# Two heads' score products of the shared query tile on quarters of the TensorE array

## The chip, the core and the metric

One core of a Trainium2 chip runs the whole program. The metric is device time in microseconds (us), the median of several executions. The engines are TensorE (PE, with its weight loads shown apart as PEld), VectorE (DVE), ScalarE (ACT), GpSimd (POOL) and SyncE (SP), which issues the DMAs.

## The reference

Attention with pooled queries, then two feed-forward layers. Only the attention is touched by the change.

```python
B, H, S, D = q.shape                      # 2, 8, 1152, 64
q_pool = q.reshape(B, H, S // 2, 2, D).mean(axis=3)      # 576 queries a head
scores = q_pool @ k.transpose(0, 1, 3, 2) / sqrt(D)      # 576 x 1152 a head
attn = exp(scores - max); attn = attn / (sum + 1e-9)
x = attn @ v                              # tokens x 512 after the heads are joined
...
x = (P(h) / Q(h)) @ w_out,  h = x @ w_in                  # d_ff 2048
x = (silu(xn @ w_gate) * (xn @ w_val)) @ w_out2           # d_ff 1536, xn = rms norm of x
```

## The kernel before

**Pairs and tiles.** The 16 heads are worked in 8 pairs. A head has 576 queries, which are four full tiles of 128 and a rest of 64. The rests of both heads of a pair lie together in one *shared tile*, so a pair has 9 tiles: four of head 0, the shared one (t = 4), four of head 1. Over the kernel there are 72 tiles, numbered i = 9 pr + t; the shared ones are 4, 13, 22, 31, 40, 49, 58 and 67. `TILES` (lines 572 to 577) lists for each tile the heads whose queries it holds (`parts`, with the first column in `qT`) and where its columns go (`dests`).

**One tile.** Queries and keys stand transposed in `qT` and `kT`. A head has 64 dimensions, so `kT` has half of the key blocks on partitions 0 to 63 (row half 0) and the rest on 64 to 127 (row half 1), and `qT` has the queries on both. Step AB (`f_qk(0)`, line 748) makes four products of 64 rows by 128 columns, each with 256 moving columns: row half 1 into PSUM bank 1, row half 0 into bank 0, twice. Step C (`f_qk(1)`) makes one of 128 columns in row half 0 into bank 2. A float32 product is two matmul instructions, so a full tile is 8 and 2 matmuls on line 754, each with a weight load. Then DVE takes the row maximum over all three banks (line 783, "red" below; it depends on both AB and C), ACT the exponential (line 789, "exp"), PE transposes it in 64-row pieces back into the same PSUM tile (line 804: step T, and one piece, T2, which waits for the copy out of bank 0), and ACT or DVE copies it to `pt` (lines 836, 839). Once a head's tiles are done, nine accumulating steps "AV" (line 907) multiply by v, in two column halves of the array.

**The shared tile before.** Its weights are 128 columns for each head: head 0's 64 rest queries with 64 zero columns behind, head 1's with 64 zero columns ahead (`qn` was cleared there at line 559). Both heads' products accumulate into the same 128 PSUM partitions (`start` on the first, `stop` on the second), so the zeros keep the heads apart. That is 16 matmuls in AB and 4 in C.

**Order.** The order on PE in the attention is written out by hand (`seq`, lines 1001 to 1013). For two tiles a (even) and b (odd), a *slot* below, it is AB of a, T2 of the tile before, C of a, AB of b, C of b, up to five AV steps, T of a, T of b, T2 of a. Other PE work (transposes of k and q on line 702, of the reciprocals on 940 and 954) goes between by time. Even shared tiles (4, 22, 40, 58) fall in slots without AV, odd ones (13, 31, 49, 67) in slots with four AV steps. Everything else is ordered by a planner (`order`, line 329): each operation has an engine or a choice of engines, a price in ns, a key, and what it depends on; the planner plays the engines forward with these prices and for each engine issues the ready operation that can begin first, with the key deciding among those within 80 ns. Each engine then runs its queue in that order. The planner also fits in the conversion of the feed-forward weights (lines 171 to 232: on ACT, DVE and POOL) wherever an engine would be free. It prices AB at 870 and C at 220 for each head in the tile, so 1740 and 440 for a shared tile, and 100 for a change between the PE modes that it names `rows` and `columns`.

**After the attention**, the first feed-forward layer starts with projections of its first two units (line 498), planned together with the attention; the rest of both layers is planned by a second call of `order`.

Of the kernel before, what the change touches and what calls it, by code (L numbers as in the profile page):

```python
# [19 lines left out]
def attention_moe_moe2_kernel(  # L20
# [29 lines left out]
    HALF = SQ % 128  # L50
    NFULL = SQ // 128
# [14 lines left out]
    def T(tag, shape, dtype=F32, space=None):  # L66
        pool(tag, BUFS.get(tag, 1), space)
        return pools[tag].tile(shape, dtype, tag=tag, name=tag)
# [348 lines left out]
    PE, DVE, ACT, POOL = "PE", "DVE", "ACT", "POOL"  # L417
# [89 lines left out]
    def banked(accesses, g, ins, also=None):  # L507

        ins = ins.ins
        for o in range(3):  # L510
            for other in accesses[o]:
                if other.engine != ins.engine:
                    if o != g and other is not also:
                        tc.declare_no_dep(ins, other, reason="another bank")
                    else:
                        tc.add_manual_dep(ins, other.name, after, reason="the same bank")
        accesses[g].append(ins)
# [39 lines left out]
    tail = [slice(0, HALF), slice(HALF, 2 * HALF)]  # L557
# [12 lines left out]


    TILES = []
    for t in range(NFULL):
        TILES.append(([(0, t * 128)], [(0, t * 128, 0, 128)]))
    TILES.append(([(0, NFULL * 128), (1, 0)], [(0, NFULL * 128, 0, HALF), (1, NFULL * 128, HALF, HALF)]))
    for t in range(NFULL):
        TILES.append(([(1, (t + 1) * 128)], [(1, t * 128, 0, 128)]))
    NT = len(TILES)

    QW = SQ // 2  # L580
# [17 lines left out]
    def op_any(ways, key, deps=(), bufs=()):  # L598
        eng, c, fn = ways[0]
        return Op(eng, c, key, fn, deps, bufs, ways[1:])  # L600
# [9 lines left out]
    kT, qT, kT_op, qT_op, v_op, v_tile, kq_buf, v_buf = ({} for _ in range(8))  # L610
# [123 lines left out]
    def tile_ops(i):  # L734
        pr, t = divmod(i, NT)
        parts, dests = TILES[t]
        ps = s_ps[i % 2]
        key = i * TS
        e = {}
        nb, pb = Buf("nm"), Buf("p")  # L740
        if t == 0:
            sum_buf[pr] = Buf("sums")
        sb = sum_buf[pr]


        ORDER_QK = [[(1, 1, 0, 256), (0, 0, 0, 256), (1, 1, 256, 512), (0, 0, 256, 512)], [(0, 2, 512, 640)]]

        def f_qk(n_):
            fresh = {}
            for a, j, x0, x1 in ORDER_QK[n_]:  # L750
                rows = slice(64 * a, 64 * a + 64)
                c = x0 % 512
                for n, (h, c0) in enumerate(parts):
                    ins = nc.tensor.matmul(  # L754
                        ps[:, j, c:c + x1 - x0],
                        lhsT=qT[2 * pr + h][rows, c0:c0 + 128],
                        rhs=kT[2 * pr + h][rows, x0:x1],
                        start=(n == 0),
                        stop=(n == len(parts) - 1),
                    )  # L760
                    banked(bank[i % 2], j, ins)
                    fresh.setdefault(j, []).append(ins.ins)
            for j in fresh:
                bank[i % 2][j][:] = fresh[j]

        deps, bufs = [], []
        for h, c0 in parts:
            deps += kT_op[2 * pr + h]
            deps += [o for (x0, x1), o in qT_op[2 * pr + h] if x0 < c0 + 128 and x1 > c0]
            bufs += kq_buf[2 * pr + h]  # L770
        o_qk = []
        for n_, (js, c) in enumerate((((0, 1), 870), ((2,), 220))):
            free = [o for j in js for o in lo_op.get((i - 2, j), ())]
            o_qk.append(Op(PE, c * len(parts), key + n_, lambda n_=n_: f_qk(n_), [*deps, *free], bufs))
            o_qk[-1].mode = "rows"
        tile_pe[i] = {"AB": o_qk[0], "C": o_qk[1]}

        def scores():
            return ps.rearrange("p g n -> p (g n)")[:, 0:S]

        def f_red():
            e["nm"] = T("nm", [128, 1])
            nc.vector.tensor_reduce(out=e["nm"], in_=scores(), op=ALU.max, axis=AX.X, negate=True)  # L783

        def f_exp():
            if pr not in sums:
                sums[pr] = T("sums", [128, NT])
            e["p"] = T("p", [128, S])
            nc.scalar.activation(  # L789
                e["p"], scores(), AF.Exp, bias=e["nm"], scale=1.0, accum_out=sums[pr][:, t:t + 1]  # L790
            )

        o_red = Op(DVE, 1350, key + -2500, f_red, o_qk, [nb])
        o_exp = Op(ACT, 1430, key + 2400, f_exp, [o_red], [nb, pb, sb])
        sum_op.setdefault(pr, []).append(o_exp)

        NB = NKT - 1

        def one_T(r, j, also=None):
            g, c = (2, 64 * r) if j == NB else (r, 64 * j)
            rows = slice(64 * r, 64 * r + 64)
            ins = nc.tensor.transpose(ps[:, g, c:c + 64], e["p"][rows, 128 * j:128 * j + 128], ident[rows, rows])  # L804
            banked(bank[i % 2], g, ins, also)

        def f_T():
            one_T(1, NB)
            for j in range(NB):
                one_T(0, j)  # L810
                one_T(1, j)

        def f_T2():
            one_T(0, NB, e["copied"].ins)


        OUTS = [(0, slice(0, NB), 0), (1, slice(0, NB), 1), (2, slice(NB, NKT), None)]

        def f_out(n_, copy):
            g, js, half = OUTS[n_]  # L820
            src = ps[:, g, 0:64 * NB if half is not None else 128]
            for h, o, s0, n in dests:
                if (pr, h) not in pt:
                    pt[pr, h] = T("pt", [128, NKT, SQ])
                to = pt[pr, h][:, js]
                if half is None:
                    banked(bank[i % 2], g, copy(to[:, 0, o:o + n], src[:, s0:s0 + n]))
                elif s0 <= 64 * half < s0 + n:
                    o_ = o + 64 * half - s0
                    ins = copy(to[:, :, o_:o_ + 64], src.rearrange("p (j n) -> p j n", n=64))  # L830
                    banked(bank[i % 2], g, ins)
                    if g == 0:
                        e["copied"] = ins

        def by_act(to, src):
            return nc.scalar.activation(to, src, AF.Copy)  # L836

        def by_dve(to, src):
            return nc.vector.tensor_copy(to, src)  # L839

        o_T = Op(PE, 560, key, f_T, [o_exp], [pb])
        o_T.mode = "rows"
        for h, *_ in dests:
            if (pr, h) not in pt_buf:
                pt_buf[pr, h] = Buf("pt")
        for n_ in range(3):
            half = OUTS[n_][2]
            hs = [h for h, o, s0, n in dests if half is None or s0 <= 64 * half < s0 + n]
            w = 64 * NB if half is not None else 128
            n2 = 150 * (len(hs) - 1)  # L850
            done = op_any(
                [(ACT, 70 + 1.09 * w + n2, lambda n_=n_: f_out(n_, by_act)), (DVE, 80 + 1.16 * w + n2, lambda n_=n_: f_out(n_, by_dve))],
                key + 3300 + 300 * n_, [o_T if half is not None else o_T2], [pt_buf[pr, h] for h in hs],
            )
            if n_ == 0:
                o_T2 = Op(PE, 60, key + 300, f_T2, [done], [pb])
                o_T2.mode = "rows"
                tile_pe[i].update(T=o_T, T2=o_T2)
            lo_op[i, OUTS[n_][0]] = [done]
            for h in hs:  # L860
                pt_op.setdefault((pr, h), []).append(done)
# [168 lines left out]
    for u in FINE:  # L1030
        free = [o for g in range(3) for o in lo_op[NP * NT - 2 + u, g]]
# [463 lines left out]
```

## Time and profile before

| | |
|---|---|
| median of 3 executions | 757.92 us (756.67 to 759.8) |
| the profiled execution's own time | 756.91 us |
| its span from first to last instruction | 755.1 us |
| mean granted TensorE clock | 0.988 |
| attention stage, to where line 498 begins on PE | about 291 us |
| matmul instructions on line 754 | 800, 160 of them in the 8 shared tiles |

The profile is of one execution, and durations are read from it; 1.8 us of its time lie outside the span. A matmul's end is modelled, so starts are more exact than ends. A timeline row merges neighbouring instructions of one kind and gives their start, how long they took together and their count (x16). "[1.80 <-PE hid L754]" says that the engine sat idle 1.80 us before that row, and what ended the wait.

### The profile page before, as it was taken

Reading aid. Unit: us, or ns where it says so; the run is one execution under the profiler, and the core shown is the slowest. Engines: PE = TensorE matmul, PEld = TensorE weight load, DVE = VectorE, ACT = ScalarE, POOL = GpSimd, SP = SyncE. Lnnn points to the kernel's source line nnn. Section 1 sums busy time; section 2 is a strip of 40 time slices with the busy share of each in tenths; the row PEclk is TensorE's granted clock in tenths of the full one; section 3 lists DMA queues with packets and bytes.
Section 4 is the critical chain, followed back from the end, with each engine's and each line's share of the span. In section 5 each row is a group of like instructions: output and inputs, shape, how many; then the busy total and the mean of one; then the engine's idle time right before and its main releaser. Section 6 shows DMA issues by size and latency. Waiting matters only on the chain.

```text
span 755.1 us, 13099 instructions
## 1 busy us (share of the span) xinstructions
PE 704.8 (93%) x5257; PEld 613.3 (81%) x5257; DVE 561.4 (74%) x713; ACT 402.9 (53%) x641; POOL 279.5 (37%) x247
## 2 busy tenths in 40 slices
PE   7998889898989999889999989889999999999997
PEld 6766666666666767889989989888999899989996
DVE  5799998888898763887896777967758435864844
ACT  4666767776776663998764835605523322312210
POOL 3033645655674000434432352316435223512500
PEclk9999999999999999999999999999999999999999
DMA  6443656566562110222203204000123302330103
GB/s 204 142 134 120 184 174 219 192 222 191 192 223 86 50 52 2 72 96 94 74 29 125 94 6 140 29 28 1 43 98 112 111 29 85 113 111 29 56 1 125
DMA packets 51596, 77.13 MB, mean 102 GB/s; under 512 B 4176, under 2 KB 33872, under 8 KB 51536
## 3 DMA queue, kind: packets, MB, share of 16 engines
q1 hardware_dynamic: 51536, 76.30, 31.2%
q8 instruction: 41, 0.67, 0.4%
q14 instruction: 19, 0.16, 0.1%
HBM read 61.87 MB, written 14.42 MB: 101 GB/s over the span
## 4 chain that ended last, share of the span: by engine, by line
PE 60%; DVE 20%; ACT 9%; issue 7%; POOL 2%; DMA 1%; SPq 0%; DVEq 0%; POOLq 0%; ACTq 0%
PE hid L498 24%; PE accp L498 16%; PE hid L754 7%; PE av L907 6%; PE hid L804 4%; ACT p L789 3%; DVE nm L783 3%; DVE pt L839 2%; DVE m_p L1131 1%; DVE m_q L1110 1%; DVE wc L176 1%; PE prep L702 1%; DVE wc L186 1%; DVE wc L180 1%; ACT m_p L1097 1%
## 5 line engine op out<-in xcount | busy, mean ns | idle before, releaser
L498 PE MATMUL hid<-x_hi,win_hi 128*128 128x384 f32 x480 | 162.3, 338 | 5.8 <-issue 2.7
L498 PE MATMUL hid<-x_lo,win_hi 128*128 128x384 f32 x480 | 161.5, 336 | 0.0
L498 PE MATMUL hid<-x_hi,win_lo 128*128 128x384 f32 x480 | 161.2, 336 | 0.0
L754 PE MATMUL hid<-kT,qT 64*128 64x256 f32 (+1 forms) x800 | 107.4, 377 | 2.8 <-DVE pt L839 2.3
L789 ACT ACTIVATE p<-hid,nm 128x1152 f32<-128x1152 f32 x72 | 87.8, 1221 | 37.4 <-DVE nm L783 37.3
L783 DVE TENSOR_REDUCE nm<-hid 128x1 f32<-128x1152 f32 x72 | 94.6, 1349 | 13.5 <-PE hid L754 12.6
L498 PEld LDWEIGHTS hid<-x_hi,win_hi 128*128 128x128 f32 x480 | 90.6, 189 | 8.7 <-issue 5.6
L754 PEld LDWEIGHTS hid<-kT,qT 64*128 64x128 f32 x800 | 86.0, 194 | 10.2 <-DVE pt L839 4.2
L498 PEld LDWEIGHTS hid<-x_lo,win_hi 128*128 128x128 f32 x480 | 90.7, 189 | 1.2 <-DVE x_lo L1303 0.3
L498 PEld LDWEIGHTS hid<-x_hi,win_lo 128*128 128x128 f32 x480 | 90.7, 189 | 0.0
L804 PEld LDWEIGHTS hid<-ident,p 64*128 64x128 f32 x1296 | 53.1, 141 | 40.4 <-ACT p L789 23.5
L804 PE MATMUL hid<-ident,p 64*128 64x64 f32 x1296 | 67.7, 232 | 16.4 <-ACT p L789 14.5
L1145 POOL TENSOR_TENSOR g_lo<-m_p,g_hi 128x1152 fp32r<-128x1152 f32 (+1 forms) x20 | 47.0, 2358 | 88.0 <-ACT g_hi L1142 88.0
L498 PE MATMUL accp<-g_hi,wout_hi 128*128 128x384 f32 x192 | 66.1, 344 | 11.5 <-DVE acc L1200 10.0
L907 PE MATMUL av<-pt,vn 128*64 128x288 f32 x576 | 76.7, 411 | 0.0
L836 ACT ACTIVATE pt<-hid 128x512 f32<-128x512 f32 (+2 forms) x132 | 54.5, 438 | 33.3 <-PE hid L804 32.2
L839 DVE COPY pt<-hid 128x512 f32<-128x512 f32 (+1 forms) x92 | 54.4, 607 | 20.4 <-PE hid L804 20.1
L171 ACT ACTIVATE wc<-wraw 128x512 f32<-128x512 f32 x68 | 45.9, 675 | 38.9 <-POOL wout_lo L204 17.2
L199 POOL TENSOR_SCALAR win_hi<-wc 128x512 fp32r<-128x512 f32 x25 | 16.1, 645 | 134.4 <-PE hid L498 105.7
L498 PE MATMUL accp<-g_lo,wout_hi 128*128 128x384 f32 x192 | 64.9, 338 | 0.2 <-POOL g_lo L1145 0.2
L498 PE MATMUL accp<-g_hi,wout_lo 128*128 128x384 f32 x192 | 64.7, 337 | 0.0
L907 PEld LDWEIGHTS av<-pt,vn 128*64 128x64 f32 x576 | 38.6, 136 | 26.3 <-issue 1.0
(121 smaller groups left out, 1277.7 us busy)
## 6 DMA issues: line engine op xcount, KB each, us to landing
wraw<-in_moe_w_out_dram SPq DMA_DIRECT2D x28, 512.0 KB, 3.5
far<-spill SPq DMA_DIRECT2D x23, 512.0 KB, 3.7
wraw<-in_moe_w_in_dram SPq DMA_DIRECT2D x16, 512.0 KB, 4.2
wraw<-in_moe_w_gate_dram SPq DMA_DIRECT2D x12, 512.0 KB, 3.6
wraw<-in_moe_w_val_dram SPq DMA_DIRECT2D x12, 512.0 KB, 3.9
kn<-in_k_dram SPq DMA_DIRECT2D x16, 288.0 KB, 3.8
vn<-in_v_dram SPq DMA_DIRECT2D x16, 288.0 KB, 3.0
qn<-in_q_dram SPq DMA_DIRECT2D x16, 256.0 KB, 3.3
```

The costliest lines, as they stand in the source:

```text
L171: nc.scalar.activation(c.bitcast(F32), wt["raw", n][:, :, 1].bitcast(F32), AF.Abs, scale=2.0**-112)
L176: nc.vector.tensor_scalar(c, c, 3, None, op0=ALU.logical_shift_left)
L199: eng.tensor_scalar(hi, w_float(n), 1.0, 1.0, op0=ALU.mult, op1=ALU.mult)
L498: ins = nc.tensor.matmul(dst, lhsT=a[x], rhs=b[y], start=first and i == 0 and p == 0, stop=last and i == n - 1 and p == 2,)
L754: ins = nc.tensor.matmul(ps[:, j, c:c + x1 - x0], lhsT=qT[2 * pr + h][rows, c0:c0 + 128], rhs=kT[2 * pr + h][rows, x0:x1], start=(n == 0), ...
L783: nc.vector.tensor_reduce(out=e["nm"], in_=scores(), op=ALU.max, axis=AX.X, negate=True)
L789: nc.scalar.activation(e["p"], scores(), AF.Exp, bias=e["nm"], scale=1.0, accum_out=sums[pr][:, t:t + 1])
L804: ins = nc.tensor.transpose(ps[:, g, c:c + 64], e["p"][rows, 128 * j:128 * j + 128], ident[rows, rows])
L836: return nc.scalar.activation(to, src, AF.Copy)
L839: return nc.vector.tensor_copy(to, src)
L907: nc.tensor.matmul(e["av", h][64 * c:64 * c + 64, 0:QW], lhsT=v_tile[2 * pr + h][:, KEYS[kt], :], rhs=pt[pr, h][:, kt, c * QW:(c + 1) * QW ...
L1145: eng.tensor_sub(g_(1), p_(), g_(0).bitcast(F32))
```

## The change

In the shared tile each head's weights are cut to its own 64 columns, and each head's product goes to its own 64 PSUM partitions: head 0 to partitions 0 to 63, head 1 to 64 to 127. With the two row halves that addresses four quarters of the array (64 rows by 64 columns each). There is no accumulation over the heads any more; every product starts and stops by itself. Full tiles keep 128 columns (`whole`). The number of instructions stays the same: 16 matmuls in AB and 4 in C. The planner's price of AB and C no longer grows with the number of heads. The hand-written order `seq` is not touched, and the mode name stays `rows`.

```diff
     TILES = []
+    whole = slice(0, 128)
     for t in range(NFULL):
-        TILES.append(([(0, t * 128)], [(0, t * 128, 0, 128)]))
-    TILES.append(([(0, NFULL * 128), (1, 0)], [(0, NFULL * 128, 0, HALF), (1, NFULL * 128, HALF, HALF)]))
+        TILES.append(([(0, t * 128, whole)], [(0, t * 128, 0, 128)]))
+    TILES.append(([(0, NFULL * 128, tail[0]), (1, HALF, tail[1])], [(0, NFULL * 128, 0, HALF), (1, NFULL * 128, HALF, HALF)]))
     for t in range(NFULL):
-        TILES.append(([(1, (t + 1) * 128)], [(1, t * 128, 0, 128)]))
+        TILES.append(([(1, (t + 1) * 128, whole)], [(1, t * 128, 0, 128)]))
...
-                for n, (h, c0) in enumerate(parts):
+                for h, c0, to in parts:
                     ins = nc.tensor.matmul(
-                        ps[:, j, c:c + x1 - x0],
-                        lhsT=qT[2 * pr + h][rows, c0:c0 + 128],
+                        ps[to, j, c:c + x1 - x0],
+                        lhsT=qT[2 * pr + h][rows, c0:c0 + to.stop - to.start],
                         rhs=kT[2 * pr + h][rows, x0:x1],
-                        start=(n == 0),
-                        stop=(n == len(parts) - 1),
+                        start=True,
+                        stop=True,
                     )
...
-            o_qk.append(Op(PE, c * len(parts), key + n_, lambda n_=n_: f_qk(n_), [*deps, *free], bufs))
+            o_qk.append(Op(PE, c, key + n_, lambda n_=n_: f_qk(n_), [*deps, *free], bufs))
```

## Rows read from the trace of the kernel before

**Rows 1.** The page: span, and the chain that ended last, by engine.
```profile
span 755.1 us, 13099 instructions
...
PE 60%; DVE 20%; ACT 9%; issue 7%; POOL 2%; DMA 1%; SPq 0%; DVEq 0%; POOLq 0%; ACTq 0%
```

**Rows 2.** Busy time by stretch: attention, and all that follows.
```profile
0.00:291.00 291.00, 263.78 (x2849) 194.98 (x2850) 241.60 (x340) 196.76 (x387) 122.40 (x136) 0.98 0.48 155
291.00:755.10 464.10, 441.07 (x2409) 418.33 (x2408) 319.79 (x373) 206.19 (x255) 157.10 (x112) 0.99 0.21 69
```

**Rows 3.** Groups by line: score products and AV, with their weight loads.
```profile
L754 PE MATMUL hid<-kT,qT 64*128 64x256 f32 (+1 forms) x800 | 107.4, 377 | 2.8 <-DVE pt L839 2.3
...
L907 PE MATMUL av<-pt,vn 128*64 128x288 f32 x576 | 76.7, 411 | 0.0
...
L907 PEld LDWEIGHTS av<-pt,vn 128*64 128x64 f32 x576 | 38.6, 136 | 26.3 <-issue 1.0
```

**Rows 4.** PE's timeline in three slots: shared tile 4, full tiles, shared tile 67.
```profile
20.11 2.05 PE L754 MATMUL hid<-kT,qT 64*128 64x256 f32 x16
22.01 0.22 PE L804 MATMUL hid<-ident,p 64*128 64x64 f32 x1
22.06 1.75 PE L754 MATMUL hid<-kT,qT 64*128 64x128 f32 x14
23.74 0.66 PE L702 MATMUL prep<-ident,kn 128*128 128x128 f32 x4
25.57 0.77 PE L804 MATMUL hid<-ident,p 64*128 64x64 f32 x17 [1.17 <-ACT p L789]
...
30.39 2.65 PE L907 MATMUL av<-pt,vn 128*64 128x288 f32 x20
...
35.75 1.63 PE L754 MATMUL hid<-kT,qT 64*128 64x256 f32 x12
37.31 2.16 PE L907 MATMUL av<-pt,vn 128*64 128x288 f32 x16
...
269.25 1.08 PE L754 MATMUL hid<-kT,qT 64*128 64x256 f32 x8
270.21 0.27 PE L804 MATMUL hid<-ident,p 64*128 64x64 f32 x1
270.30 2.63 PE L754 MATMUL hid<-kT,qT 64*128 64x256 f32 x22
272.86 2.16 PE L907 MATMUL av<-pt,vn 128*64 128x288 f32 x16
```

**Rows 5.** DVE's timeline at shared tiles 4, 22, 31, 40, 58, 67.
```profile
22.82 2.62 DVE L783 TENSOR_REDUCE nm<-hid 128x1 f32<-128x1152 f32 x2 [1.80 <-PE hid L754]
...
97.42 2.62 DVE L783 TENSOR_REDUCE nm<-hid 128x1 f32<-128x1152 f32 x2 [0.33 <-PE hid L754]
...
130.49 1.36 DVE L783 TENSOR_REDUCE nm<-hid 128x1 f32<-128x1152 f32 x1 [0.89 <-PE hid L754]
...
169.63 1.52 DVE L219 SCALAR_TENSOR_TENSOR wc<-wraw,wc 128x512 uint32<-128x512 uint32 x1
171.06 2.61 DVE L783 TENSOR_REDUCE nm<-hid 128x1 f32<-128x1152 f32 x2
...
242.74 2.62 DVE L783 TENSOR_REDUCE nm<-hid 128x1 f32<-128x1152 f32 x2 [0.24 <-PE hid L754]
...
270.79 1.36 DVE L783 TENSOR_REDUCE nm<-hid 128x1 f32<-128x1152 f32 x1 [0.64 <-PE hid L754]
273.02 1.36 DVE L783 TENSOR_REDUCE nm<-hid 128x1 f32<-128x1152 f32 x1 [0.87 <-PE hid L754]
```

**Rows 6.** ACT's timeline at shared tile 31.
```profile
132.52 0.82 ACT L588 ACTIVATE xt<-av 64x288 f32<-64x288 f32 x2 [0.99 <-PE av L907]
...
134.02 1.23 ACT L789 ACTIVATE p<-hid,nm 128x1152 f32<-128x1152 f32 x1
```

**Rows 7.** Busy time and granted clock (third from the end) around tile 22; PE's timeline there.
```profile
93.00:96.00 3.00, 3.00 (x27) 2.81 (x25) 2.47 (x4) 1.32 (x3) 2.01 (x3) 0.50 0.88 306
...
93.61 3.22 PE L754 MATMUL hid<-kT,qT 64*128 64x256 f32 x16
```

More of the change, by code (lines that the diff above doesn't have):

```diff
@@ L766, in tile_ops @@
         deps, bufs = [], []
-        for h, c0 in parts:
+        for h, c0, to in parts:
             deps += kT_op[2 * pr + h]
-            deps += [o for (x0, x1), o in qT_op[2 * pr + h] if x0 < c0 + 128 and x1 > c0]
+            deps += [o for (x0, x1), o in qT_op[2 * pr + h] if x0 < c0 + to.stop - to.start and x1 > c0]
             bufs += kq_buf[2 * pr + h]
```

## The prediction

> **What bounds the kernel now.** I read the page first. The chain that ended last is 60% PE, 20% DVE and 9% ACT [rows 1], so no one engine sets the time alone. The busy times by stretch split it: up to 291 us, where the attention ends, PE is busy 263.8 us and DVE 241.6; in the 464 us behind, PE is busy 441 [rows 2]. The change touches only the attention, and whatever it saves there moves the start of a stage that it does not touch. In the attention the work passes from engine to engine: scores on PE, maximum on DVE, exponential on ACT, transposes on PE, copies on DVE and ACT. PE waits for the exponential (1.17 us ahead of T of tile 4 [rows 4]) and DVE waits for the scores (1.80 us in the same slot [rows 5]). So I do not price the change by PE's busy time but slot by slot, by what the maximum and the transposes wait for there.
>
> The groups by line show what a product costs [rows 3]: 800 matmuls of the scores with 107.4 us between them, the 8 shared tiles holding 160 of them. PE's timeline shows one shared tile beside full ones [rows 4]. In the slot of tile 4, AB of the shared tile starts at 20.11 and T2 behind it at 22.01: 1.90 us. In the slot of tile 66, a full one, it is 270.21 - 269.25 = 0.96. The shared tile pays for two heads one after the other in each half of the array's rows.
>
> **The change part by part.**
>
> *AB and C in quarters.* Removed: no instruction; 16 and 4 matmuls stay. What can change is how many run side by side. Today 8 further matmuls cost 1.90 - 0.96 = 0.94 us, 0.12 us each, with two row halves running together. Whether column halves run together too is seen in AV, which uses two of them: 20 matmuls take 2.65 us, 16 take 2.16 [rows 4], so one costs (2.65 - 2.16)/4 = 0.12 us, while its mean duration is 411 ns [rows 3]. It streams 288 columns where the score product streams 256, at the same price per instruction, so two column halves run together as two row halves do. The trace has no product on a quarter. The bounds: four quarters together make AB of the shared tile as long as that of a full tile, 0.96; if the column halves take turns, it stays at 1.90. The nearest row is AV's, so I take the first, about 1.0.
>
> *Even shared tiles (4, 22, 40, 58).* DVE's maximum for tile 4 starts 22.82 - 20.11 = 2.71 us after its AB [rows 4, 5]; for full tile 66, where DVE also waited for PE, 270.79 - 269.25 = 1.54. The difference, 1.17 us, is what the second head costs on this path (0.94 in AB, the rest in C). On PE alone less is gained, since C of an even tile shares the array with AB of the odd one behind it: the 14 matmuls from 22.06 take 23.74 - 22.06 = 1.68 until the next work, the 12 of a full slot 37.31 - 35.75 = 1.56.
>
> *Odd shared tiles (13, 31, 49, 67).* From C of the even tile to the first AV there are 22 matmuls and 272.86 - 270.30 = 2.56 us; a full slot has 12 and 1.56 [rows 4]. The second head costs 1.00 us on the path through AV to T.
>
> *Added: changes of the array's shape.* T2 and full tiles run on 64*128, the quarters on 64*64. Where the shape changes today, the next block starts 0.07 us ahead of the modelled end of the block before (22.06 + 1.75 = 23.81 against 23.74); where it stays, 0.15 us ahead (20.11 + 2.05 = 22.16 against 22.01) [rows 4]. That is 0.08 us. On top the new block has to fill: AV's 20 matmuls take 2.65 where 20 x 0.1225 is 2.45, so 0.2 us for start and end together. A change costs between 0.08 and 0.28; I take 0.15. An even shared tile has four changes, three of them ahead of its maximum (before AB, between AB and T2, between T2 and C); an odd one has one more than today, since AV follows it with a change anyway.
>
> *The sum.* Even: 1.17 - 3 x 0.15 = 0.72. Odd: 1.00 - 0.15 = 0.85. Four of each make 6.3 us; without the price of the changes it would be 8.7.
>
> *Whether the slots give it back.* This depends on DVE's queue. If each queue kept its order, a tile would gain no more than the wait in front of its maximum [rows 5]: tile 4 its 0.72 (of 1.80), tile 22 0.33, tile 31 0.85 (of 0.89), tile 58 0.24, tile 67 0.85 (of 0.87), and tiles 13, 40, 49 nothing, because DVE ran a weight conversion up to the maximum (tile 40: line 219 for 1.52 us until the maximum at 171.06; the other two look like it). That makes 3.0 us. But these conversions stand there because the planner saw a hole: it prices the shared scores at 1740 + 440. With 870 + 220 the maximum is ready when it looks, and the conversion goes to another hole; DVE has 291 - 242 = 49 us of them [rows 2]. The same holds for ACT at tile 31: the maximum was done at 131.85, yet the exponential begins at 134.02, behind two copies that waited for AV until 132.52 [rows 6]. With the lower price it can be issued ahead of them, worth up to 134.02 - 131.85 = 2.17 us by itself in such a slot. So 3.0 is the floor while the quarters work, and 8.7 about the ceiling. I take 6 us, close to the sum. What is late next: in even slots the copy out of bank 0 that T2 waits for, in odd ones the maximum of the even tile ahead of that of the shared one on DVE (1.36 us each).
>
> *The new prices elsewhere.* All orders of DVE, ACT and POOL in the attention are planned anew, and the second layerwise plan starts from the engines' new end times. No row prices that; I put it into the range. One event can be priced: a stretch at half clock. Around tile 22 the granted clock is 0.50, the lower of the two levels, 1.2 GHz, and the same 16 matmuls take 3.22 us in place of 2.05 [rows 7], 1.17 more. One such stretch more or less moves the time by about that.
>
> *The sum against its own time.* The profiled execution took 756.91, so 750.9; the median shown is 757.92, 1.0 above it, so 751.9 for the measured median. I predict 752.
>
> *A rule of the skill that speaks against it.* AV's weight loads take 136 ns and its matmuls follow each other at 0.1225 us with two running at once [rows 3, 4]; ten pairs with the load waited for would take 10 x (0.245 + 0.136) = 3.8 us, and the row has 2.65. The Trainium skill, "TensorE: Matmul & The Clock Gate", Part 3 (The mechanism), says that a weight load overlaps running matmuls only when its row group differs from theirs, and the two heads of one row half share it. The trace disagrees for column halves over all rows; no row shows it for quarters. What it would do here is the second rival.
>
> **The rivals.**
>
> *1. The quarters do not run together.* The row halves do, the column halves take turns, and AB stays at 1.90. Then only the changes of shape are new: four in an even tile and one in an odd one, 5 x 0.15 x 4 = 3.0 us, so 761. For it: the trace has no 64*64 product. Against it: AV.
>
> *2. Quarters run together, but each load waits for the running matmuls of its row half.* Each quarter has four passes of 0.94/4 = 0.235 us; each would pay 136 ns more, 0.54 us a tile. Even tiles keep 0.72 - 0.54 = 0.18, odd ones 0.85 - 0.54 = 0.31: 2.0 us, 756.
>
> *3. Slower: all four quarters in turn.* If products on quarters lose the overlap of the row halves as well, 16 passes of 0.235 take 3.8 us in place of 1.90, in C nothing changes, and with the changes of shape it is 8 x 1.9 + 3 = 18 us: 776. Its place is AB of the shared tile, and it decides by 0.5% once AB takes more than 1.90 + (3.8 - 3.0)/8 = 2.0 us. Against it: rows and columns overlap separately today.
>
> *4. The gain is made and given back by the new order.* Conversions that leave the holes of tiles 13, 40 and 49 land in front of another maximum or delay the copies. For it: DVE is busy 83% of the attention. Worth up to the 6 us: 756 to 759. Against it: the weights' keys rank them behind the tiles' own work when both are ready.
>
> **How the numbers follow.** A measurement of this kernel tells about 0.5%, 3.8 us, from no change. My case has a chance of 0.64: a gain of 3.0 to 8.7, 749 to 755. A larger gain through the reordered exponentials, 743 to 749, has 0.08. Rival 1 has 0.05, rival 2 0.08, rival 3 0.04, rival 4 0.11. Faster by over 0.5% (below 754.1) takes 0.59 of the first and the 0.08, 0.67. Slower (above 761.7) takes rival 3, half of rival 1 and 0.02 of rival 4, 0.09. The rest, 0.24, is the same. The range of 746 to 759 leaves out about 0.07 below and 0.12 above.
>
> **What would show it.** In the trace after, the shared tile's matmuls carry 64*64, AB with 16 of them lasts near 1.1 us, and T2 behind tile 4 starts about 1.2 us after AB in place of 1.90. The waits of DVE for line 754 shrink (1.80 in the slot of tile 4 to about 1.1), line 219 no longer stands in front of the maximum of tile 40, and line 498 begins on PE near 285 us. AB still near 1.9 means rival 1; 64*64 matmuls a load apart, rival 2; AB near 3.8, rival 3; AB short but line 498 still near 290, rival 4. The prediction is also wrong if the feed-forward stage does not simply start earlier but changes its own 464 us.

## The result

The changed kernel takes 746.95 us (median of 5 executions, 745.29 to 748.49) against 759.26 for the kernel before beside it (median of 5); the ratio is 0.9841, 95% interval 0.9817 to 0.9866. It is faster by about 12 us, twice the 6 forecast, and at the lower end of the range of 746 to 759. The profiled execution took 745.6 us with a span of 743.8, 11.3 less than before. Below, medians and ratios are of the fast executions alone: two of the twelve of the quarters in the old order (761.38 and 762.03 us), one of the quarters at the price halfway (1122.02) and one of the kernel before (865.72) are slow ones and stand in neither.

The page of the kernel after gives its span and the chain that ended last by engine, as [rows 1] did:

```profile
span 743.8 us, 13108 instructions
...
PE 62%; DVE 20%; ACT 9%; issue 6%; POOL 2%; DMA 1%; SPq 0%; DVEq 0%; POOLq 0%; ACTq 0%
```

Busy time by stretch, cut again where line 498 begins on PE (columns as in [rows 2]):

```profile
0.00:279.50 279.50, 257.62 (x2849) 185.42 (x2849) 236.20 (x350) 196.95 (x379) 123.09 (x133) 0.98 0.50 161
279.50:743.80 464.30, 441.35 (x2409) 418.62 (x2409) 320.06 (x374) 206.48 (x255) 157.51 (x113) 0.99 0.21 69
```

All of it comes from the attention, 11.5 us by these cuts; the 464 us behind it only start earlier. PE is busy 6.2 us less in the attention than in [rows 2], and DVE 5.4 less. The quarters cannot explain DVE: it has no less to do with them. This is the first sign that something else came along.

PE's timeline after, in the slots of shared tiles 13 and 58 (lines behind the edit stand one lower, 755 for 754). The 22 matmuls are two of tile 12 and all twenty of tile 13:

```profile
52.40 0.27 PE L805 MATMUL hid<-ident,p 64*128 64x64 f32 x1
52.51 1.68 PE L755 MATMUL hid<-kT,qT 64*128 64x128 f32 x22
54.12 2.16 PE L908 MATMUL av<-pt,vn 128*64 128x288 f32 x16
...
228.88 1.09 PE L755 MATMUL hid<-kT,qT 64*64 64x256 f32 x16
230.03 0.27 PE L805 MATMUL hid<-ident,p 64*128 64x64 f32 x1
230.23 1.72 PE L755 MATMUL hid<-kT,qT 64*64 64x128 f32 x14
231.88 0.66 PE L703 MATMUL prep<-ident,kn 128*128 128x128 f32 x4
```

AB of tile 58 is 16 matmuls on 64*64 in 1.09 us, where 16 on 64*128 took 2.05 and the 8 of a full tile 1.08 [rows 4]: four products run side by side. In the odd slot it is 54.12 - 52.51 = 1.61 us from C of the even tile to AV, against 2.56 before and 1.56 in a full slot [rows 4].

DVE's timeline at shared tiles 4, 13, 40 and 58, for [rows 5]:

```profile
24.37 2.62 DVE L784 TENSOR_REDUCE nm<-hid 128x1 f32<-128x1152 f32 x2 [1.70 <-PE hid L755]
...
53.55 2.61 DVE L784 TENSOR_REDUCE nm<-hid 128x1 f32<-128x1152 f32 x2
...
160.88 0.88 DVE L840 COPY pt<-hid 128x512 f32<-128x512 f32 x2
161.68 2.76 DVE L784 TENSOR_REDUCE nm<-hid 128x1 f32<-128x1152 f32 x2
...
230.14 0.76 DVE L605 TENSOR_TENSOR x_lo<-xt,x_hi 128x576 fp32r<-128x576 f32 x1 [0.16 <-POOL x_hi L592]
230.81 2.62 DVE L784 TENSOR_REDUCE nm<-hid 128x1 f32<-128x1152 f32 x2
```

The conversion on line 219 no longer stands in front of the maximum of tile 40, and the two maxima of slot 12 (a slot is named by its first tile) follow each other (x2 in one row). Tile 4 still waits 1.70 us. A part of that is the clock: it is 0.50, the lower level of 1.2 GHz, from 20.0 to 23.3 us, and the 16 matmuls take 1.78 us there in place of 1.09. Without these 0.69 us the wait would be about 1.0, by this estimate, where 1.1 was forecast. Busy time with the granted clock, and PE's row:

```profile
20.00:23.30 3.30, 2.96 (x43) 2.04 (x39) 1.38 (x2) 1.95 (x5) 0.00 (x0) 0.50 0.92 274
...
21.91 1.78 PE L755 MATMUL hid<-kT,qT 64*64 64x256 f32 x16
```

ACT's timeline at shared tile 31, for [rows 6]: the exponential of tile 31 comes right behind that of tile 30, ahead of the copies that wait for AV.

```profile
124.74 1.22 ACT L790 ACTIVATE p<-hid,nm 128x1152 f32<-128x1152 f32 x1
125.85 0.20 ACT L790 ACTIVATION_READ_ACCUMULATOR p<-hid,nm 128x1 f32 x1
125.94 1.23 ACT L790 ACTIVATE p<-hid,nm 128x1152 f32<-128x1152 f32 x1
```

### The profile page after: what moved, and what is told of

Its sections match the earlier page's. It is cut to its first block, busy times and chain, and to the rows that moved or that the text cites. A ratio compares the mean times of both kernels' runs of the same rounds, so it can differ in the third digit from the quotient of the medians.

```text
span 743.8 us, 13108 instructions
## 1 busy us (share of the span) xinstructions
PE 699.0 (94%) x5257; PEld 604.0 (81%) x5257; DVE 556.3 (75%) x723; ACT 403.4 (54%) x633; POOL 280.6 (38%) x245
## 4 chain that ended last, share of the span: by engine, by line
PE 62%; DVE 20%; ACT 9%; issue 6%; POOL 2%; DMA 1%; SPq 0%; DVEq 0%; POOLq 0%; ACTq 0%
PE hid L498 22%; PE accp L498 16%; PE hid L755 9%; PE av L908 8%; PE hid L805 4%; DVE nm L784 2%; DVE pt L840 2%; ACT p L790 2%; DVE m_p L1132 2%; DVE m_q L1111 1%; DVE wc L186 1%; PE prep L703 1%; DVE m_q L1126 1%; ACT m_p L1098 1%; DVE wc L180 1%
## 5 line engine op out<-in xcount | busy, mean ns | idle before, releaser
L790 ACT ACTIVATE p<-hid,nm 128x1152 f32<-128x1152 f32 x72 | 87.7, 1220 | 31.0 <-DVE nm L784 30.5
L755 PE MATMUL hid<-kT,qT 64*128 64x256 f32 (+3 forms) x800 | 99.9, 383 | 3.8 <-DVE pt L840 3.3
L755 PEld LDWEIGHTS hid<-kT,qT 64*128 64x128 f32 (+1 forms) x800 | 75.4, 185 | 14.1 <-DVE pt L840 4.7
L805 PE MATMUL hid<-ident,p 64*128 64x64 f32 x1296 | 69.2, 234 | 12.5 <-ACT p L790 10.1
L498 PE MATMUL accp<-g_hi,wout_hi 128*128 128x384 f32 x192 | 66.1, 344 | 11.3 <-DVE acc L1201 9.9
L840 DVE COPY pt<-hid 128x512 f32<-128x512 f32 (+2 forms) x94 | 51.7, 567 | 18.4 <-PE hid L805 18.1
```

The lines of the kernel that those rows point to most:

```text
L498: ins = nc.tensor.matmul(dst, lhsT=a[x], rhs=b[y], start=first and i == 0 and p == 0, stop=last and i == n - 1 and p == 2,)
L755: ins = nc.tensor.matmul(ps[to, j, c:c + x1 - x0], lhsT=qT[2 * pr + h][rows, c0:c0 + to.stop - to.start], rhs=kT[2 * pr + h][rows, x0:x1], ...
L790: nc.scalar.activation(e["p"], scores(), AF.Exp, bias=e["nm"], scale=1.0, accum_out=sums[pr][:, t:t + 1])
```

## The experiments

The diff does two things: it moves the products to quarters, and it lowers two prices of the planner, by which the other queues are ordered. The first question was which of the two brings the 12 us.

**Quarters alone, in the old order.** The changed kernel with the old price. The queues of DVE, ACT and POOL are then operation for operation those of the kernel before.

```diff
-            o_qk.append(Op(PE, c, key + n_, lambda n_=n_: f_qk(n_), [*deps, *free], bufs))
+            o_qk.append(Op(PE, c * len(parts), key + n_, lambda n_=n_: f_qk(n_), [*deps, *free], bufs))
```

> The quarters with the planner's old price (1740 and 440 for the shared tile), so that DVE, ACT and POOL have the order of the kernel before, operation for operation. Theory A (the quarters and the lower price each bring a part): only the waits in front of the maximum shrink, the forecast's floor of 3.0 us, so 3 to 5 us faster than before, the attention ending near 287 us. Rival B (the quarters bring it all, whatever the order): 11 to 12 us faster, the attention ending near 279. Rival C (the gain comes from another order of the queues and the quarters are worth nothing by themselves): within 1 us of before, near 291.

Measured: 754.45 us, ratio 0.9969 (0.9946 to 0.9991), 2.3 us faster. In its profile the attention ends at 286.3 (290.8 in the kernel before). Rival B falls. The 2.3 is just under theory A's 3 to 5 and the forecast's floor of 3.0, but it was measured at a lower clock than the kernel before had, which the next run takes up. DVE's timeline in the slots of tiles 13 and 40 shows what the old order leaves in the way:

```profile
53.34 1.34 DVE L784 TENSOR_REDUCE nm<-hid 128x1 f32<-128x1152 f32 x1
54.61 0.96 DVE L176 TENSOR_SCALAR wc<-wc 128x512 uint32<-128x512 uint32 x1
55.60 0.69 DVE L180 SCALAR_TENSOR_TENSOR wc<-wraw,wc 128x512 uint32<-128x512 uint32 x1
56.21 1.35 DVE L784 TENSOR_REDUCE nm<-hid 128x1 f32<-128x1152 f32 x1
...
167.89 1.52 DVE L219 SCALAR_TENSOR_TENSOR wc<-wraw,wc 128x512 uint32<-128x512 uint32 x1
169.33 2.61 DVE L784 TENSOR_REDUCE nm<-hid 128x1 f32<-128x1152 f32 x2
```

The conversions stand where the planner saw a hole, and the maximum waits behind them although its scores are ready.

**The new order alone.** The kernel before with the new price: serial products, queues as in the kernel after.

```diff
-            o_qk.append(Op(PE, c * len(parts), key + n_, lambda n_=n_: f_qk(n_), [*deps, *free], bufs))
+            o_qk.append(Op(PE, c, key + n_, lambda n_=n_: f_qk(n_), [*deps, *free], bufs))
```

> The products of before (128 columns, the two heads one after the other) with the planner's new price (870 and 220), so that DVE, ACT and POOL have the order of the kernel after. Theory A: the order is made for scores that now come about 1 us later in each of 8 tiles, and the maximum stands in the queue with nothing in front of it; the order still moves weight conversions out of the way, so the attention ends 3 to 5 us before 291, 286 to 288. Rival B (only the quarters count): no gain, 290 to 292, or a loss of some us. Rival C (only the order counts): near 280, 10 us or more faster.

Measured: 753.66 us, ratio 0.9949 (0.9932 to 0.9966), 3.9 us faster with not one product changed, as theory A had it. 2.3 and 3.9 make 6.2; together they bring 12.1.

Most of that gap goes with the clock. The executions of the quarters in the old order had a mean granted clock of 0.980, the kernel before beside them 0.987, the new price alone and both together 0.986. Where it was alike, the quarters in the old order took 749.92 us against 755.24 to 755.58 (at 0.991) and 754.14 against 760.84 (at 0.982), 5.5 and 6.7 us less. At 0.986 the new price alone took 753.25 against 757.81 (means of 5 and 8 executions), 4.6 less, and both together, in another session, 746.82 (mean of 4), 11.0 less. By these few executions the two parts about add up.

What DVE has to do goes with the order. Busy time of the attention, the quarters in the old order first, then the new order alone:

```profile
0.00:286.30 286.30, 258.21 (x2848) 183.61 (x2848) 241.56 (x340) 196.39 (x387) 122.48 (x135) 0.98 0.49 157
```

```profile
0.00:287.50 287.50, 265.36 (x2849) 196.69 (x2849) 236.77 (x350) 196.92 (x379) 122.71 (x133) 0.98 0.48 157
```

The third busy time is DVE's: 241.6 with 340 instructions in the old order, as in [rows 2], and 236.8 with 350 in the new. The planner chose other engines for some operations, and some take less time each where they now run: DVE has line 605 (604 in the second kernel) 6 times at a mean of 1116 ns in the old order, 5 times at 833 in the new.

**One column half.** As the changed kernel, with both heads' 64 columns in the same half of the array's columns.

```diff
-    TILES.append(([(0, NFULL * 128, tail[0]), (1, HALF, tail[1])], ...
+    TILES.append(([(0, NFULL * 128, tail[0]), (1, HALF, tail[0])], ...
```

> As the changed kernel, but head 1's 64 columns go to the same column half as head 0's, so that two quarters run at a time and not four; what lands on PSUM partitions 64 to 127 of the shared tile is then old data, so a part of the output is not the reference's. Same orders as the changed kernel. Theory A (the four quarters side by side are what shortens the scores): AB of the shared tile takes 1.8 to 1.9 us again, and the time is that of the new price alone within 1 us. Rival D (narrower weights or the lack of accumulation over the heads do it): AB stays near 0.95 us, and the time is that of the changed kernel.

Measured: 755.02 us, ratio 0.9972 (0.9952 to 0.9992), 1.4 above the new order alone (753.66), where 1 was expected. PE's timeline at tile 58:

```profile
231.16 2.00 PE L755 MATMUL hid<-kT,qT 64*64 64x256 f32 x16
233.09 0.27 PE L805 MATMUL hid<-ident,p 64*128 64x64 f32 x1
```

AB takes 2.00 us with narrow weights and no accumulation. So it is the second column half, running beside the first, that shortens it. This is also what rival 1 would have looked like: at the like clock of 0.986 this kernel takes 756.05 us (mean of 4) against 753.25, 2.8 more, and rival 1 priced the changes of shape at 3.0.

**The price halfway, for both kinds of products**, 1305 and 330, same order in both:

```diff
+            o_qk.append(Op(PE, c * (1 + len(parts)) // 2, key + n_, ...
```

> The quarters with a price halfway (1305 and 330). Theory A: the planner still sees a smaller hole, and the gain lies between that of the old price and that of the new one, 5 to 10 us. Rival C (the order is a draw that no price steers): anything from 0 to 12 us, with no regard to the order of the prices.

> The products of before with the price halfway (1305 and 330). Theory A (a lower price lets the maximum stand free of conversions, and pays even where the scores still come late): between before and the new price alone, 0 to 4 us faster than before, the attention ending at 287 to 291. Theory E (every order is a draw with a spread of some us, whatever the price says of the scores): anywhere from 282 to 294.

Measured: quarters 749.12 us, 0.9898 (0.9875 to 0.9922), 7.7 us faster than before; serial products 747.88 us, 0.9878 (0.9844 to 0.9913), 9.2 us faster. The second is the surprise of the study, outside both expectations (its attention ends at 279.6): the products of the kernel before, untouched, give three quarters of the gain with one number of the planner changed. By the four prices tried with serial products the order is close to a draw with a spread of some 9 us, and the kernel before had the poorest of the four. With this order the quarters did not make the kernel faster by a measurable amount; in the profiles their shared slots are 3.0 us shorter and the other slots 2.0 longer (table below), with 13.7 us at half clock in the attention against 3.4. The clock hides a part of what they bring: their mean granted clock was 0.981 against 0.988, and at 0.986 there is one execution of either, 746.65 and 748.54 us.

**Prices near the new one**, a tenth lower and a fifth higher, and the serial products with the latter's order:

```diff
+            o_qk.append(Op(PE, c * 9 // 10 if len(parts) > 1 else c, key + n_, ...
```

```diff
+            o_qk.append(Op(PE, c * 6 // 5 if len(parts) > 1 else c, key + n_, ...
```

> As the changed kernel, with the price of the shared tile's AB and C a tenth lower (783 and 198). The products are the same; only the order of DVE, ACT and POOL differs. Theory A: the hole in front of the maximum is closed either way, and the attention ends within 1.5 us of the changed kernel's 279.5, leaving half-clock stretches aside. Theory E: it ends anywhere from 276 to 286.

> As the changed kernel, with the price of the shared tile's AB and C a fifth higher (1044 and 264). Theory A: within 1.5 us of the changed kernel, as for the lower price. Theory E: the attention ends anywhere from 276 to 286.

> The products of before with the price of 1044 and 264 and so with the order of the fastest kernel yet, operation for operation. Theory A+E (quarters and order each count): 4 to 8 us slower than the quarters with this order, 748 to 752. Theory E alone: 744 to 746.

Measured: 747.10 us, 0.9855 (0.9818 to 0.9892) for the lower price; 743.98 us, 0.9828 (0.9795 to 0.9861) for the higher, the fastest kernel of the study, though its interval overlaps that of the changed one. Their attention ends at 279.0 and 276.6, so theory A's 1.5 us around 279.5 holds for the first alone, though both have 6.8 us at half clock and the changed kernel 13.7. Measured further: 753.65 us, 0.9933 (0.9889 to 0.9977) for the serial products in its order, a little above the 748 to 752 of A+E and far from E alone. Near the new price the orders differ by some 3 us, and the quarters bring 13.0 - 5.1 = 7.9 us over serial products in the same order. The profile of the serial kernel also has 469.8 us behind the attention, at a clock of 0.98, where that of the quarters has 464.3 at 0.99; but at the like clock of 0.986 the executions, 753.65 and 754.38 against 745.71, are 8.3 apart.

**T2 behind C.** In a slot with an even shared tile, C follows AB directly.

```diff
-            seq += [a["AB"], *([was["T2"]] if was else []), a["C"], b["AB"], b["C"]]
+            t2 = [was["T2"]] if was else []
+            if i % NT == NFULL:
+                seq += [a["AB"], a["C"], *t2, b["AB"], b["C"]]
+            else:
+                seq += [a["AB"], *t2, a["C"], b["AB"], b["C"]]
```

> As the changed kernel, but in a slot with an even shared tile T2 of the tile before comes behind C, so that AB and C on quarters follow each other and two of the four changes of the array's shape go. By the forecast's 0.15 us a change that is 2 x 0.15 x 4 = 1.2 us less in the shared slots, and C no longer waits for the copy that T2 waits for. It also makes the planner order the other queues anew; theory E puts the total anywhere within 4 us of the changed kernel, theory A within 2 us of it.

Measured: 748.18 us, 0.9876 (0.9846 to 0.9906). The shared slots are 1.1 us shorter than in the changed kernel (59.6 against 60.7), but that is not the 1.2 expected: the four odd ones, where the order on PE stayed, went from 30.1 to 28.3, and the four even ones, where it was changed, from 30.6 to 31.3, with 2.6 us more at half clock, worth about 0.9 at the 1.17 for 3.22 us of [rows 7]. Slot 58, at full clock in both, went from 7.37 to 7.50. The other slots are 2.2 longer in the new order that came with it. So neither the whole nor the even slots show a gain from fewer changes of shape.

**The attention without conversions.** To see the quarters without the draw, all loads and conversions of the feed-forward weights wait for the last exponential, once with serial products and the old price, once with quarters and the new price:

```diff
-    later = sum_op[0][4]
+    later = sum_op[NP - 1][NT - 1]
```

> The kernel before with every load and conversion of the feed-forward weights held back until the last exponential, so that the attention runs alone and DVE, ACT and POOL have only its own work. The whole takes longer, since the conversions follow behind. It is read beside the next kernel by where line 498 could begin, the end of the last tile's copies. Theory A (the quarters are worth what the paths through the slots say, the conversions only hide it): the attention is 265 to 280 us long.

> The changed kernel with the conversions held back in the same way. Theory A: the attention is 5 to 8 us shorter than with the serial products, the forecast's sum of 6.3, 0.6 to 1.0 us in each of the 8 shared slots and nothing in the others. Theory E (most of the gain is the order in which conversions fall): under 3 us.

Measured: 836.88 and 834.98 us, one execution each, longer as meant. PE's timeline, serial products first, in the slots 22 (even) and 30 (odd), each with the start of the slot behind it:

```profile
87.75 2.10 PE L754 MATMUL hid<-kT,qT 64*128 64x256 f32 x16
...
95.14 0.44 PE L754 MATMUL hid<-kT,qT 64*128 64x256 f32 x2
...
116.96 1.08 PE L754 MATMUL hid<-kT,qT 64*128 64x256 f32 x8
...
124.70 0.65 PE L754 MATMUL hid<-kT,qT 64*128 64x256 f32 x4
```

```profile
89.46 1.09 PE L755 MATMUL hid<-kT,qT 64*64 64x256 f32 x16
...
96.26 0.44 PE L755 MATMUL hid<-kT,qT 64*128 64x256 f32 x2
...
118.07 1.08 PE L755 MATMUL hid<-kT,qT 64*128 64x256 f32 x8
...
125.05 0.49 PE L755 MATMUL hid<-kT,qT 64*128 64x256 f32 x2
```

The even slot goes from 7.39 to 6.80 us, 0.59 less, the odd one from 7.74 to 6.98, 0.76 less; slots 40 and 58, and 12, 48 and 66, repeat these lengths. Four of each make 5.4 us. This is not the quarters alone, since the two kernels differ in the price too, and their queues of DVE and ACT are not the same. Where the queues are, in the kernel before and the quarters in its order, the slots 58 and 66, at full clock, go from 7.39 to 6.80 and from 7.74 to 6.81. The expectation for the whole was missed all the same: the last exponential begins only 2.1 us earlier, and line 498 on PE 3.7 (274.8 for 278.5). Until the last exponential the quarters' run spent 13.7 us at half clock, from 13.4 to 16.9 and from 20.3 to 30.5 us, the serial one 3.4. At 1.17 us for every 3.22 at half clock [rows 7] that is 3.7 us, an estimate, and with it the 2.1 would be 5.8. The slots that follow the odd shared ones are partly shorter (7.95 to 7.63) and partly longer (7.27 to 8.01); in them DVE and ACT have traded copies of `kT` and `qT`, but that this is the reason is not shown.

The slots of all kernels, from one start of AB to the next, summed over the 8 with a shared tile and the 28 others, with the microseconds at half clock in the attention, one profile each:

| kernel | price | shared | others | half clock | ratio |
|---|---|---|---|---|---|
| before, serial | 2 x | 67.8 | 215.0 | 10.2 | 1 |
| quarters | 2 x | 64.0 | 214.2 | 13.7 | 0.9969 |
| serial | 1.5 x | 66.1 | 205.7 | 3.4 | 0.9878 |
| quarters | 1.5 x | 63.1 | 207.7 | 13.7 | 0.9898 |
| serial | 1.2 x | 64.3 | 210.8 | 3.4 | 0.9933 |
| quarters | 1.2 x | 57.8 | 211.5 | 6.8 | 0.9828 |
| serial | 1 x | 66.8 | 212.5 | 13.7 | 0.9949 |
| after, quarters | 1 x | 60.7 | 211.1 | 13.7 | 0.9841 |

In every pair of one order the quarters shorten the shared slots, by 3.8, 3.0, 6.5 and 6.1 us. The others move by up to 9.3 us, and that goes with the order. Shared and others together are 4.6, 1.0, 5.8 and 7.5 us shorter with the quarters, which have 3.5, 10.3, 3.4 and 0 us more at half clock; with these priced as above, the quarters are worth about 5.9, 4.7, 7.0 and 7.5 us, an estimate from one profile each. The change of shape ahead of an even shared tile falls into the slot before: with the quarters in the old order slot 38 went from 6.98 to 7.18 and slot 56 from 6.70 to 6.90.

## Why the prediction came out as it did

**Quarters together: right.** AB takes 1.09 us, "about 1.0" was forecast. Rivals 1 and 3 fall, and with one column half left out the 1.9 us return. Rival 2 falls too: with the loads waited for, AB would be near 1.5. The Trainium skill's rule ("TensorE: Matmul & The Clock Gate", Part 3, The mechanism) that a load overlaps only with matmuls of another row group is not what this trace shows for quarters either: 16 loads and 16 matmuls, two quarters in each row half, fit into 1.09 us.

**The changes of shape: right in all, not each.** PE's timeline at tile 58, the kernel before first, then the quarters in the same order:

```profile
240.04 0.28 PE L804 MATMUL hid<-ident,p 64*128 64x64 f32 x1 [0.34 <-DVE pt L839]
240.04 2.10 PE L754 MATMUL hid<-kT,qT 64*128 64x256 f32 x16
241.98 0.22 PE L804 MATMUL hid<-ident,p 64*128 64x64 f32 x1
242.04 1.75 PE L754 MATMUL hid<-kT,qT 64*128 64x128 f32 x14
```

```profile
236.58 0.27 PE L805 MATMUL hid<-ident,p 64*128 64x64 f32 x1 [0.34 <-DVE pt L840]
236.78 1.09 PE L755 MATMUL hid<-kT,qT 64*64 64x256 f32 x16
237.81 0.27 PE L805 MATMUL hid<-ident,p 64*128 64x64 f32 x1
238.01 1.72 PE L755 MATMUL hid<-kT,qT 64*64 64x128 f32 x14
```

Ahead of AB the change costs 236.78 - 236.58 = 0.20 us, where both began at once before. Between AB and T2 there are 1.03 us, 0.07 more than the 0.96 of a full tile [rows 4]. Between T2 and C there are 0.20, against 0.06 before: 0.14. The three make 0.41, where 3 x 0.15 was taken. In an odd slot the one change costs 1.61 - 1.56 = 0.05.

**The sum of the shared slots: about right.** 0.72 and 0.85 were forecast; 0.59 and 0.76 were measured without conversions, and 0.59 and 0.93 in the slots 58 and 66 of the old order. On the way to the maximum of tile 58 the changed kernel needs 230.81 - 228.88 = 1.93 us from AB, the kernel before 242.74 - 240.04 = 2.70 [rows 5], 0.77 more. In the old order it is 238.95 - 236.78 = 2.17, because DVE comes to the maximum only behind line 605:

```profile
238.27 0.76 DVE L605 TENSOR_TENSOR x_lo<-xt,x_hi 128x576 fp32r<-128x576 f32 x1
238.95 2.62 DVE L784 TENSOR_REDUCE nm<-hid 128x1 f32<-128x1152 f32 x2
```

In whole executions of like clock the quarters alone gave 5.5 and 6.7 us, where the sum was 6.3.

**The floor and what lies above it: the floor was too low.** The quarters in the old order gave 2.3 us by the ratio, near the floor of 3.0, but that is the lower clock: the slots of the attention are 4.6 us shorter, and at like clock it is 5.5 and 6.7. So the waits ahead of the maxima do not bound the gain. The slot of tile 49, for which the floor had nothing, went from 9.41 to 8.70. For tile 13 the reason named holds: its maximum stands behind conversions, and its slot went only from 9.14 to 8.98. In the new order the conversions ahead of the maxima of tiles 13, 40 and 49 went elsewhere, and the exponential of tile 31 moved ahead of the copies.

**"No row prices that; I put it into the range": the step that failed.** The new order was taken as something that could give back up to 6 us (rival 4) and otherwise as width of the range. It gave 3.9 us by itself (4.6 at like clock), and other orders of the same serial products give 5.1 and 9.2. The sum had the quarters' part, about 6, and put the order's at nothing, so the gain came out at twice the forecast. 8.7 was no ceiling, and rival 4 had the wrong sign. That 746.95 still lies above 746, the lower end, is owed to the width of the range and not to a term of the sum. Nothing in the trace of before said that its own order was a poor one; DVE's 241.6 us of work, 5 more than in the new orders, could only be seen as too much beside another order.

**The stage behind: right.** 464.1 us before and 464.3 after, by the cuts shown.

What stays open: what makes one order better than another, and why the quarters had a lower mean granted clock than the serial products at the old price (0.980 against 0.987) and at the price halfway (0.981 against 0.988), but not at the others. DVE's work is 236 to 237 us in each profile with a price of 1, 1.2 or 1.5, while the other slots range from 205.7 to 212.5, so it is not that alone. And the half-clock stretches fall elsewhere in every profile (0 to 13.7 us of the attention), so single profiles of one order differ by some us: the new order alone and the one-column-half kernel have the same queues and AB of about 2 us, and end the attention at 287.5 with 13.7 us at half clock and at 283.9 with none.

## What to carry to other kernels

A price in a scheduler is a part of the change: run the new price with the old code, and the new code with the old price, before the gain is put down to the hardware. Then look at the granted clock before the parts are added up. Here they gave 2.3 and 3.9 us alone and 12 together, which looks as if one needed the other; at like clock it was 5.5 to 6.7 and 4.6 against 11.0. Where orders are planned from prices, scan a few of them first; one number gave 9 us with no product changed. And products of 64 rows and 64 columns can be worth placing on quarters of the array: here 16 matmuls, four at a time, took 1.09 us, as 8 did two at a time (1.08), with the changes of shape on top.

## What the runs showed of the hardware

Four float32 products of 64 rows by 64 columns run side by side at full pace: 16 matmuls of 256 columns in 1.09 us, 0.07 us each, against 0.12 with two at a time. Changing between 64*64 and 64*128 cost 0.07 to 0.20 us at tile 58, 0.05 in an odd slot. At half clock the same 16 took 1.78 us.
